# Attention with agents and a cosine FFN: one more lot of queries in the second and third burst of a batch

## The chip, the cores and the metric

One core of one Trainium2 chip runs the kernel. The metric is the time of one execution on the device, in microseconds; of the kernel before three runs are shown, 1187.72 to 1188.53 us, median 1188.37 us.

## The reference

For each of 4 batches there are 12480 queries, keys and values of 128 elements, and 49 agent vectors. `sm(a, b)` is the softmax over b of the scaled products of a and b.

```python
a2k = sm(agents, k)          # 49 x 12480
agent_v = a2k @ v            # 49 x 128
q2a = sm(q, agents)          # 12480 x 49
x = q2a @ agent_v            # attention output, 12480 x 128 per batch
h = x @ w_in                 # 49920 x 2048
out = (h * cos(h)) @ w_out   # 49920 x 128
```

## The kernel before

The queries of all batches are worked in 52 groups of 960, 13 a batch. In place of x, the kernel folds `agent_v @ w_in` into a matrix `a` for each batch (`project`, line 334), so that one product of the transposed softmax weights `pT` with `a` gives h.

**The steps.** The main loop (lines 807 to 829) has 16 steps a group, 832 in all. Step n computes two matmuls of 113 x 480 into a PSUM tile `ph` of two banks (L771, three such tiles), a Sin on ACT into `c` (L774), a scalar_tensor_tensor on DVE that makes `r` = (c - 1) * h (L780, called the cubic step here), and, four steps later (`LAG`), two matmuls of `r` with `w_out` (L796), accumulated over eight steps in a PSUM tile `one`. The last of eight adds two matmuls with `b1` and `b2` (L792, L793) and a copy to `osb` (L798); every 16 steps a group of the output goes to memory. There are two tiles `one`; one of them holds these output sums nearly all the time, the other serves everything else.

**The lots.** All that a later group or batch needs is done in between, in lots that hang on steps. A lot of **queries** (`query_parts`, line 415) loads 480 KB of transposed queries on SP (tile `xt`, three buffers), multiplies them by the agents (8 matmuls at L139, each in two passes, so 16 in the trace) into the free `one`, copies the scores to `e` (L432: on ACT, or on DVE where `by_vector` is set), takes the maxima on DVE (L436) and subtracts them on POOL (L438). A lot of **keys** (`scores`, line 221) is alike, with a running maximum on DVE. A lot of **values** (`add_values`, line 490) adds the exponentials to `es` on POOL (L283), loads twice 240 KB on SP (tile `vt`, six buffers), multiplies them by the exponentials of the keys (L297, 16 passes) into the free `one`, and adds that to `sums` on DVE (L305; the first lot copies, L303). A **turned** group (`query_turned`, line 501) transposes a group's weights on PE (L505), copies on ACT (L509) and writes `pT` on POOL (L512, L513). Each of the steps outside the bursts that are free takes at most one lot: `extra` (line 621) looks for the next of three steps in eight (five where `dense`).

**The bursts.** Exp and Sin need different tables on ACT, so the Exps are gathered: three bursts a batch, at steps 109, 133 and 157 from the batch's start (`BURSTS`, line 527). At a burst ACT loads the Exp table, runs one Exp over a piece of 4 or 5 query groups (L480) and one over 4 or 5 lots of keys (L273), and loads the Sin table at the next L774. DVE then sums the query groups (`query_sum`, L483), and five steps on computes their inverse (`query_inverse`, L487 and L488). For the six steps of a burst PE, DVE and ACT keep the order in which the code is written (`as_traced`, line 89).

`fill` (line 667) puts up to three lots into a burst and reserves its first three steps: the first lot whole at the burst's own step, two of the sums and then the second lot one step on (the other sums behind it), the matmuls of the third lot at the second step and the rest of it at the third. A query within a burst has its copy on DVE. Here the burst's steps put a lot ahead of `second_product`, and the cubic step of step n comes at step n + 1, after `first_product`.

Lines 708 to 735 hand out the lots of batch `b`'s keys and values (b = 1 to 3) and of the coming queries. `fresh[k]` lists the queries for burst k: four for the first, three that are left of five for the second (two go out before it), and the first two of the next batch for the third. `vs` lists the values: four for the second burst, four and then five for the third. The string of line 713 says in which order `fill` gets them; what it does not take is spread over the steps up to the next burst, or put every two to six steps after the third. After the values come the total, the folding, the inverse and the four projections of the batch (lines 736 to 742), and then the lots of the next batch's keys.

Of the kernel before, what the change touches and what calls it, by code (L numbers as in the profile page):

```python
# [41 lines left out]
def agent_attention_cos_ffn(ctx, tc, qT, kT, v, agT, w_in, w_out, outT):  # L42
# [338 lines left out]
    with ExitStack() as pools:  # L381
# [239 lines left out]
        def extra(n, f, *args, dense=False):  # L621


            while n in taken or (n - LAG) % NP not in ((1, 2, 3, 4, 5) if dense else (1, 3, 5)):
                n += 1
            taken.add(n)
            plan(n, f, *args)
            return n
# [5 lines left out]
        def spread_out(todo, t, end):  # L634

            for i, lot in enumerate(todo):
                t = extra(t, *lot) + 1
                if i + 1 < len(todo):
                    t += max(0, (end - t) // (len(todo) - i - 1) - 1)
            return t  # L640
# [14 lines left out]
        def burst(t, piece, keys=None):  # L655
            assert t + 4 < piece[0] * STEP - 10
            windows.add(t)
            plan(t, query_exp, piece)
            if keys:
                plan(t, pinned_exp, *keys)  # L660
            sums.extend((n, t) for n in piece)
            plan(t + 5, query_inverse, piece)

        def scored(piece, *how):
            return [(query, n, piece, *how) for n in piece]

        def fill(at, todo):

            taken.update(range(at, at + 3))
            parts = [in_parts(*todo.pop(0)) for _ in range(min(3, len(todo)))]  # L670
            if parts:
                plan(at, list, parts[0])
            early_plan(at + 1, summed, at, 2)
            if len(parts) > 1:
                early_plan(at + 1, list, parts[1])
            early_plan(at + 1, summed, at, 9)
            for x, n in zip(parts[2:], range(at + 2, at + 9)):
                early_plan(n, next, x)
                (early_plan if n + 1 < at + 5 else plan)(n + 1, list, x)
# [7 lines left out]
        for b in range(1, NB):  # L687
            o, ps = (b - 1) * PER, pieces[b - 1]

            def valued(k):  # L690
                return [(add_values, ab[b], g) for g in range(lots[k][0], sum(lots[k]))]

            qs, ks = scored(ps[0])[ahead:], [(ab[b].scores, g) for g in range(3 if b == 1 else 0, NG)]
            both = []
            while qs or ks:
                both += ks[:3] + qs[:1]
                ks, qs = ks[3:], qs[1:]
            t = spread_out(both, t, o + BURSTS[0] - 14)
            plan(t, ab[b].top)
            t = extra(t, ab[b].across)  # L700
            t = extra(t + 1, ab[b].spread)
            assert t < o + BURSTS[0], (t, o)
            for g, n in lots:
                plan(t, ab[b].shift, g, n, nc.gpsimd)
            nxt = scored(pieces[b][0], False, True)[:2]
            ahead = len(nxt)
            fresh = [scored(ps[1], False, True), scored(ps[2], False, True), nxt]
            for k, at in enumerate(BURSTS):
                at += o
                burst(at, ps[k], (ab[b], *lots[k]))  # L710
                vs, qs = valued(k - 1) if k else [], fresh[k]
                todo = []
                for x in ("qqqqqqq", "vq", "vq")[k]:
                    z = vs if x == "v" else qs
                    if z:
                        todo.append(z.pop(0))
                fill(at, todo)
                t = at + 6
                if k == 2:
                    vs += valued(2)  # L720
                qs, todo = todo, []
                qs += [x for x in fresh[k] if x not in qs]
                qs = [x[:3] if x[0] is query else x for x in qs]
                while vs or qs:
                    todo += qs[:1] + vs[:1]
                    vs, qs = vs[1:], qs[1:]
                if k == 0:
                    todo += [x[:3] for x in fresh[1][:2]]
                    del fresh[1][:2]
                end = o + BURSTS[min(k + 1, 2)] - 4  # L730
                for i, x in enumerate(todo):
                    t = extra(t, *x, dense=k == 2) + (2 if k == 2 else 1)
                    assert k == 2 or x[0] is not query or t < o + BURSTS[k + 1], (t, o, k)
                    if k < 2 and i + 1 < len(todo):
                        t += max(0, (end - t) // (len(todo) - i - 1) - 1)
            plan(t, ab[b].total)
            t = extra(t, ab[b].folded) + 1
            t = extra(t, ab[b].inverse) + 1
            i = b % 2
            for c in range(DFF // 512):  # L740
                t = extra(t, ab[b].project, c, a[i], dense=True) + 1
            t = extra(t, ab[b].project_out, wio, b1[i], b2[i], dense=True)
            plan(t, ab[b].judge)
            t += 1
            assert t < o + PER + 2, (t, o + PER)
# [229 lines left out]
```

## Time and profile before

| What | us |
|---|---|
| Median of three runs | 1188.37 |
| The profiled execution's own time | 1186.01 |
| Its span | 1184.2 |
| PE / DVE / ACT / POOL busy | 1129.3 / 1073.1 / 970.0 / 349.9 |
| Cubic steps on DVE (L780), 832 of them, busy | 916.4 |
| Sin on ACT (L774), 832 of them, busy | 785.4 |

The profile is that of one execution. The page sums it up by engine and by line; a timeline lists the instructions of an engine in order of time (start, duration, engine, line, operation, tiles, count, and in brackets the idle time before it with what ended it); windows give the busy time of every engine in a stretch of the span, with the number of instructions, the mean granted clock of TensorE (1.00 is 2.4 GHz) and the share of the DMA engines. Matmuls that follow each other overlap in the records, so a duration of one is longer than its place in the stream.

### The profile page before, as it was taken

How to read it: one execution, taken by the hardware profiler on the slowest of the kernel's cores; microseconds unless marked ns; L12 is line 12 of the kernel's file. 1: busy time of each engine (PE TensorE's matmuls, PEld its weight loads, DVE VectorE, ACT ScalarE, POOL GpSimd, SP SyncE). 2: the span in 40 equal slices, each digit the busy share in tenths (PEclk: the TensorE clock that was granted, in tenths of full speed). 3: DMA queues.
4: the chain of work that ended last, by engine and by line, in shares of the span. 5: the costliest groups of instructions: out<-in, count | busy, mean ns of one | idle time of the engine just before them, and what ended most of it. 6: DMA issues, size and time to landing. Idle time of an engine off the chain costs nothing.

```text
span 1184.2 us, 17390 instructions
## 1 busy us (share of the span) xinstructions
PE 1129.3 (95%) x6359; PEld 917.0 (77%) x6359; DVE 1073.1 (91%) x1220; ACT 970.0 (82%) x1201; POOL 349.9 (30%) x387
## 2 busy tenths in 40 slices
PE   8899999999999999998899999999999999998997
PEld 7678889777777888887677888878777777666774
DVE  6879999999889999998789999999878999999997
ACT  2568888888778888888778888888777899998996
POOL 1022221743313231373313231263332232122320
PEclk9899999999999999999899999999989999998999
DMA  9983233333341223233342222233331000000001
GB/s 340 246 244 100 85 100 100 101 100 95 106 134 50 84 68 100 68 101 100 100 134 68 84 70 88 82 97 106 95 100 35 34 17 34 34 18 34 18 34 37
DMA packets 39190, 107.74 MB, mean 91 GB/s; under 512 B 4344, under 2 KB 4728, under 8 KB 39096
## 3 DMA queue, kind: packets, MB, share of 16 engines
q1 hardware_dynamic: 39096, 106.55, 28.4%
q8 instruction: 52, 0.85, 0.3%
q14 instruction: 42, 0.34, 0.1%
HBM read 80.97 MB, written 25.56 MB: 90 GB/s over the span
## 4 chain that ended last, share of the span: by engine, by line
PE 67%; DVE 17%; ACT 8%; issue 4%; DMA 3%; POOL 0%; SPq 0%; ACTq 0%; DVEq 0%
PE ph L771 25%; PE one L796 22%; DVE r L780 14%; PE one L139 10%; ACT c L774 5%; PE one L297 3%; PE one L792 2%; PE one L793 1%; PE one L505 1%; DMA vt<-w_out 1%; DMA vt<-v 1%; PE one L342 1%; ACT osb L798 1%; ACT L480 1%; ACT s L273 1%
## 5 line engine op out<-in xcount | busy, mean ns | idle before, releaser
L780 DVE SCALAR_TENSOR_TENSOR r<-c,ph 128x960 fp32r<-128x960 f32 x832 | 916.4, 1148 | 62.9 <-ACT c L774 56.6
L774 ACT ACTIVATE c<-ph 128x960 f32<-128x960 f32 x832 | 785.4, 980 | 111.5 <-PE ph L771 99.0
L771 PE MATMUL ph<-pT,a 113*128 113x480 f32 x1664 | 540.7, 405 | 22.9 <-DVE r L780 21.6
L796 PE MATMUL one<-r,w 128*128 128x480 f32 x1664 | 504.0, 391 | 2.0 <-ACT osb L798 1.7
L771 PEld LDWEIGHTS ph<-pT,a 113*128 113x128 f32 x1664 | 293.0, 191 | 137.8 <-DVE r L780 73.3
L796 PEld LDWEIGHTS one<-r,w 128*128 128x128 f32 x1664 | 311.7, 192 | 55.5 <-issue 4.8
L139 PEld LDWEIGHTS one<-ag,xt 128*120 128x120 f32 x1408 | 162.8, 187 | 14.1 <-DVE sums L303 4.2
L139 PE MATMUL one<-ag,xt 128*120 128x49 f32 x1408 | 159.3, 266 | 5.4 <-DVE sums L303 2.9
L496 POOL TENSOR_TENSOR p<-e,rz 120x392 f32<-120x392 f32 x51 | 43.2, 851 | 328.0 <-PE one L505 252.5
L513 POOL TENSOR_TENSOR pT<-p,pT 49x480 fp32r<-49x480 f32 x102 | 124.1, 1217 | 7.8
L438 POOL TENSOR_TENSOR e<-e,mx 120x392 f32<-120x392 f32 x49 | 41.3, 843 | 212.8 <-DVE mx L436 212.3
L512 POOL CAST pT<-p 49x480 fp32r<-49x480 f32 x102 | 59.3, 582 | 115.0 <-ACT p L509 110.3
L798 ACT COPY osb<-one 128x480 f32<-128x480 f32 x104 | 57.9, 557 | 4.0 <-PE one L796 4.0
L297 PE MATMUL one<-vt,s 120*49 120x128 f32 (+1 forms) x624 | 44.6, 288 | 5.2 <-DVE sums L305 5.2
L297 PEld LDWEIGHTS one<-vt,s 120*49 120x49 f32 (+1 forms) x624 | 34.7, 135 | 18.0 <-issue 8.1
L283 POOL TENSOR_TENSOR es<-es,s 120x392 f32<-120x392 f32 x36 | 36.8, 1021 | 37.3 <-ACT s L273 35.7
L269 POOL TENSOR_TENSOR s<-s,mxb 120x1568 f32<-120x1568 f32 (+1 forms) x9 | 31.5, 3531 | 34.1 <-DVE mxb L265 34.1
L793 PE MATMUL one<-pT,b 113*128 113x480 f32 x104 | 40.3, 388 | 0.0
L792 PE MATMUL one<-pT,b 113*128 113x480 f32 x104 | 40.3, 387 | 0.0
L235 ACT COPY s<-one 120x392 f32<-120x392 f32 x36 | 17.5, 487 | 20.7 <-PE one L139 20.7
L432 ACT COPY e<-one 120x392 f32<-120x392 f32 x34 | 16.5, 487 | 20.3 <-PE one L139 20.3
L505 PEld LDWEIGHTS one<-ident,p 120*113 120x113 f32 x204 | 28.6, 179 | 4.7 <-ACT a L343 0.9
(105 smaller groups left out, 551.1 us busy)
## 6 DMA issues: line engine op xcount, KB each, us to landing
xt<-qT SPq DMA_DIRECT2D x52, 480.0 KB, 3.5
vt<-v SPq DMA_DIRECT2D x104, 240.0 KB, 3.5
outT<-osb SPq DMA_DIRECT2D x51, 480.0 KB, 2.6
xt<-kT SPq DMA_DIRECT2D x46, 480.0 KB, 3.5
c<-kT SPq DMA_DIRECT2D x6, 480.0 KB, 7.5
vt<-w_in SPq DMA_DIRECT2D x8, 256.0 KB, 7.1
vt<-w_out SPq DMA_DIRECT2D x8, 256.0 KB, 7.6
outT<-osb SPq DMA_DIRECT2D x2, 240.0 KB, 2.8
```

The lines of the kernel that those rows point to most:

```text
L139: mm = nc.tensor.matmul(ps[:, t, :], xt[:, t * TT:(t + 1) * TT], ag[:, b, :], start=True, stop=True)
L297: mm = nc.tensor.matmul(po[h * HI:h * HI + width], e[:, x * NA:x * NA + width], vt[:, x, :], start=(t == 0 and first), stop=(t == HT - 1 a ...
L496: nc.gpsimd.tensor_mul(p_in[n % 2].rearrange("p t (h a) -> p h t a", h=2)[:, :, :, :NA], e.rearrange("p (h t) a -> p h t a", h=2), rz_of.p ...
L512: nc.gpsimd.tensor_copy(pT[own, c], p[own])
L513: nc.gpsimd.tensor_sub(pT[other, c], p[own], pT[own, c].bitcast(F32))
L771: nc.tensor.matmul(ph[:, j, :CH], ai[:, f], pTs[q % 3][:, c], start=True, stop=True)
L774: nc.scalar.activation(cos, h, AF.Sin, bias=HALF_PI, scale=1.0)
L780: nc.vector.scalar_tensor_tensor(r, cos, 1.0, h, op0=ALU.subtract, op1=ALU.mult)
L792: nc.tensor.matmul(po, b1[k], pTs[q % 3][:, c], start=False, stop=False)
L793: nc.tensor.matmul(po, b2[k], pTs[q % 3][:, c], start=False, stop=False)
L796: nc.tensor.matmul(po, w1[:, f, :], r[:, j, :], start=(f == 0), stop=(f == NF - 1))
L798: nc.scalar.copy(osb[:, c * CH:(c + 1) * CH], po)
```

## The change

The strings of line 713 for the second and the third burst get a query ahead. `fill` then receives three lots in place of two at these bursts: a query at the burst's own step, values one step on, a query at the second and third step. What is left for the steps after is one query less; all that is handed out after it takes the place before its own. No lot is added or left out. The copy of the query that moves into a burst goes from ACT to DVE (`by_vector`).

```diff
@@ -710,7 +710,7 @@
                 burst(at, ps[k], (ab[b], *lots[k]))
                 vs, qs = valued(k - 1) if k else [], fresh[k]
                 todo = []
-                for x in ("qqqqqqq", "vq", "vq")[k]:
+                for x in ("qqqqqqq", "qvq", "qvq")[k]:
                     z = vs if x == "v" else qs
                     if z:
                         todo.append(z.pop(0))
```

## Rows read from the trace of the kernel before

**Rows 1.** The page: busy times by engine (part 1), issues of DMA (part 6).

```profile
PE 1129.3 (95%) x6359; PEld 917.0 (77%) x6359; DVE 1073.1 (91%) x1220; ACT 970.0 (82%) x1201; POOL 349.9 (30%) x387
...
xt<-qT SPq DMA_DIRECT2D x52, 480.0 KB, 3.5
```

**Rows 2.** Windows of eight steps at a burst; columns: stretch, length, busy by engine, clock.

```profile
503.87:519.05 15.18, 14.33 (x86) 11.33 (x86) 14.00 (x21) 13.46 (x13) 13.21 (x13) 1.00 0.42 131
257.86:272.50 14.64, 13.12 (x71) 10.91 (x71) 12.69 (x18) 13.52 (x14) 9.20 (x10) 0.88 0.24 71
539.18:554.85 15.67, 12.63 (x66) 10.59 (x66) 12.54 (x18) 13.65 (x14) 9.19 (x10) 0.89 0.22 67
823.67:840.04 16.37, 13.33 (x71) 11.29 (x71) 13.11 (x18) 13.66 (x15) 9.23 (x10) 0.90 0.21 63
294.11:311.25 17.14, 14.12 (x83) 12.05 (x84) 12.81 (x20) 13.84 (x13) 5.88 (x6) 0.90 0.36 115
577.00:595.39 18.39, 15.37 (x80) 12.92 (x81) 13.07 (x20) 14.03 (x13) 5.89 (x6) 0.81 0.33 107
861.56:880.30 18.74, 16.90 (x83) 14.55 (x84) 12.83 (x20) 13.94 (x13) 5.88 (x6) 0.73 0.35 106
```

**Rows 3.** Windows of eight steps outside the bursts.

```profile
954.59:963.36 8.77, 8.42 (x34) 5.92 (x34) 8.60 (x9) 7.74 (x10) 0.00 (x0) 1.00 0.14 56
...
554.85:566.03 11.18, 11.11 (x73) 9.30 (x73) 9.81 (x10) 8.40 (x10) 0.84 (x1) 1.00 0.41 132
272.50:283.14 10.64, 10.57 (x68) 8.75 (x68) 9.69 (x11) 8.41 (x10) 0.84 (x1) 1.00 0.42 140
283.14:294.11 10.97, 10.07 (x69) 7.77 (x68) 9.69 (x11) 9.09 (x12) 5.20 (x6) 1.00 0.31 90
...
322.59:333.34 10.75, 10.75 (x82) 8.43 (x81) 9.43 (x12) 7.71 (x9) 0.00 (x0) 1.00 0.56 182
333.34:343.48 10.14, 10.14 (x71) 8.17 (x71) 9.24 (x11) 8.12 (x10) 4.38 (x5) 1.00 0.35 102
311.25:322.59 11.34, 11.02 (x75) 8.74 (x75) 9.62 (x11) 8.86 (x11) 5.21 (x6) 1.00 0.30 87
595.39:607.04 11.65, 11.33 (x78) 9.04 (x78) 9.73 (x11) 8.87 (x11) 5.22 (x6) 1.00 0.28 86
```

**Rows 4.** Timeline, second burst of batch 2, DVE and PE; last column: idle before.

```profile
541.80 1.03 DVE L483 TENSOR_REDUCE rz<-e 120x8 f32<-120x392 f32 x2 [1.27 <-ACT e L480]
...
540.59 1.88 PE L139 MATMUL one<-ag,xt 128*120 128x49 f32 x16 [0.99 <-DVE sums L303]
...
546.79 0.68 PE L771 MATMUL ph<-pT,a 113*128 113x480 f32 x2 [2.06 <-DVE r L780]
```

**Rows 5.** Timeline, first burst of batch 2, PE and DVE.

```profile
505.55 1.88 PE L139 MATMUL one<-ag,xt 128*120 128x49 f32 x16 [0.66 <-DVE e L432]
...
512.30 0.56 DVE L432 COPY e<-one 120x392 f32<-120x392 f32 x1
...
513.45 3.27 DVE L780 SCALAR_TENSOR_TENSOR r<-c,ph 128x960 fp32r<-128x960 f32 x3
```

**Rows 6.** Timeline, third burst of batch 1, PE and DVE.

```profile
295.51 1.94 PE L297 MATMUL one<-vt,s 120*64 120x128 f32 x16 [1.72 <-DVE sums L305]
...
297.51 0.29 DVE L305 TENSOR_TENSOR sums<-sums,one 113x128 f32<-113x128 f32 x1 [2.05 <-PE one L297]
...
300.90 0.56 DVE L432 COPY e<-one 120x392 f32<-120x392 f32 x1 [2.17 <-PE one L139]
...
303.45 5.41 DVE L780 SCALAR_TENSOR_TENSOR r<-c,ph 128x960 fp32r<-128x960 f32 x5
```

**Rows 7.** L487: durations (ns min/median/max), then DVE and POOL at one of them.

```profile
L487 DVE TENSOR_SCALAR rz<-rz x12: 106/178/1000, 115.8 to 1075.1; 120x32 f32<-120x32 f32 x7, 120x40 f32<-120x40 f32 x4, 120x8 f32<-120x8 f32 x1
...
836.79 1.00 DVE L487 TENSOR_SCALAR rz<-rz 120x32 f32<-120x32 f32 x1
...
835.23 2.52 POOL L513 TENSOR_TENSOR pT<-p,pT 49x480 fp32r<-49x480 f32 x2
```

## The prediction

> **What bounds the kernel now.** I began with the busy times of the page: PE 95% of the span [rows 1], DVE and ACT less. Such a share says little of a burst, so I cut the DVE row into blocks of eight steps, each from the start of the cubic step L780 at one n to the one eight later, and asked for the busy times and the granted clock of each block. The plan's arithmetic (lines 690 to 745) says which lots stand in a block.
>
> Outside the bursts [rows 3] the blocks are regular. With no lot a block takes 8.77 us; that is eight cubic steps on DVE back to back. With three lots of values it takes 10.75, with two of values and a turned group 10.14; one query and one lot of values make 10.64, the same with a turned group 10.97 (11.34 and 11.65 after the third burst). PE is busy for 92 to 100% of all of these. So a block with two or more lots is paced by PE, and a lot costs what it costs there: values (10.75 - 8.77) / 3 = 0.66, and a query 10.97 - 8.77 - 0.66 = 1.5.
>
> A block that starts at a burst [rows 2] is another thing. The first burst of a batch, which holds three queries, takes 15.18 us with PE busy for 14.33 of it at granted clock 1.00 (batch 2; batch 3 gives the same, batch 1 half a microsecond more). The second burst holds less work, one lot of values and one query and a turned group, and takes 14.64, 15.67 and 16.37 in the three batches: PE is busy for 13.12, 12.63 and 13.33, at a mean clock of 0.88 to 0.90. The third takes 17.14, 18.39 and 18.74 at 0.90, 0.81 and 0.73. A mean of 0.88 over 14.64 us is 0.12 / 0.5 x 14.64 = 3.5 us at the lower of the two levels, 1.2 GHz.
>
> What holds PE up is seen in the order of the second burst [rows 4]. While ACT loads the Exp table, runs two Exps and loads Sin again, the only cubic steps that can run are those whose cosine is there. PE waits 0.99 us for the DVE copy that frees the PSUM buffer of the values (there is one such buffer: the other of the two holds the output sums), and then 2.06 us for an L780, because the ph buffers are full and it has no lot left. DVE has nothing either for 1.27 us, until the first Exp. In the first burst [rows 5] the same place has a third query; PE waits 0.66 us and nothing like the 2.06, and DVE pays for the third query behind two cubic steps: its copy begins at 512.30 and, the reduce done, the next cubic step at 513.45, so 1.15 us.
>
> **The change part by part.** Six bursts change, two in each of three batches; the first burst does not.
>
> *Second burst, inside.* The query now comes ahead of the values, and a second query two steps on. Each query issues one load of 480 KB on SP, eight matmuls, on DVE a PSUM copy in place of ACT's and a reduce (1.15 us together), and a POOL subtraction. The first copy and reduce fall into the 1.27 us in which DVE waits for Exp; the values' add, 0.29 us in [rows 6], follows the first two sums. DVE goes on when the cosine of the next step is there, as now; the second query then costs 1.15 us behind the next two cubic steps, as in the first burst. On PE its eight matmuls, 1.88 us in [rows 4], take the place of the 2.06 us wait. I price the block by the nearest rows: the first burst's 15.18 and 0.2 for the turned group that it lacks, 15.4 in every batch. Bounds: 15.0 with the values lighter than the query that they stand for, and 17.5, the worst of now (16.37) with the whole 1.15 on top. Against now: +0.8, -0.3, -1.0, together **-0.5**. The load is an early one: SP already holds the loads of the queries ahead, three buffers deep, and after the first burst it serves three queries in this spacing; I cost it at nothing, covered by those buffers, and at up to a load's 3.5 us [rows 1] per burst if they run dry; no load was waited for there in the first burst, so I stay at nothing. Loads of values that stand behind it on SP have six buffers; outputs have two.
>
> *Second burst, outside.* In the block after the burst the remaining query moves up to the place of the one that left, and a lot of values to the place after: one of each, as now. So 10.6, which takes 0.6 off in batch 2 alone (11.18 now, behind the slow clock). The block after that loses its query and keeps one lot of values and a turned group: 8.77 + 0.66 = 9.43 against 10.97, -1.54 in each of three batches, **-4.6**. If only DVE counted, the gain would be the reduce alone, under half of the 1.15 above; that is the lower bound.
>
> *Third burst, inside.* Here the last lot of values of the stretch before falls on the burst's own step, ahead of Exp, and the burst's first lot has to wait for its buffer: 1.7 us on PE [rows 6]. That stays, with a query as the one that waits. In batch 1 DVE now adds the second lot's sums at 297.51, waits 2.17 us for the query's matmuls, copies at 300.90, and starts the next cubic step only at 303.45. After: the query's matmuls start at 295.5 and end at about 297.7, copy and reduce to 299.1, two sums to 300.1; the values' matmuls run beside these, their add ends at 300.6, three sums to 302.0, then the cubic step, 1.45 us sooner. The new query's 1.15 comes two steps on. So 17.14 - 1.45 + 1.15 = 16.8 at full clock. The wait of 1.7 us that comes ahead of the low clock is still there, so I take 17.0 in all three. Bounds 15.7 (the new query hidden: 17.14 - 1.45) and 19.9 (18.74 and 1.15). Against now: -0.1, -1.4, -1.7, together **-3.3**.
>
> *Third burst, outside.* The next block swaps its query for values: 10.14 against 11.34, 11.65 and 11.34, **-3.9**. All later lots move up one place; at the end of the chain one place of values is gone, 0.66 a batch, **-2.0**. Total, inverse and the four projections of the next batch only come earlier, by two to six steps; the work that needs them starts long after, so nothing for that.
>
> The sum: -0.5 - 0.6 - 4.6 - 3.3 - 3.9 - 2.0 = **-14.9 us**. The profiled execution took 1186.0 us, 1184.2 of it span, so 1171.1 for it; the median of the runs shown lies 2.4 us above it, at 1188.4, so **1174 us** with some of the rounding against me.
>
> *A rule against it.* The reciprocal's first half (L487) reads and writes SBUF on DVE five steps into each burst. It took 1.00 us at 836.79 and ended 0.04 us after POOL's pair of L513 did, where 0.178 is its median [rows 7]. The change puts one more POOL subtraction ahead of that place. If L487 meets a POOL instruction in all six bursts, 6 x (1.00 - 0.18) = 4.9 us. The Trainium skill, page "SBUF — State Buffer", section "SBUF: two separate sides", says why: VectorE and GpSimd share a pair of ports that one instruction holds to its end while the other is blocked. By that rule the sum would be -10.0; by the rows, in which some bursts already pay for it, -14.9.
>
> **The rivals.** *The third lot only stacks up (1184).* Each block keeps its time and clock of now and DVE pays 1.15 on top: 6 x 1.15 = +6.9 inside in place of -3.8, and -11.1 outside: -4.2. For it: DVE's own sum rises, as a copy moves from ACT to it. Against it: the first burst [rows 2] does more in less time.
>
> *The port pair decides (1178.5).* As priced above.
>
> *One free PSUM buffer makes it slower (1198).* Three lots in a burst pass through one buffer. The second query's matmuls wait for the values' add, which stands on DVE behind two sums that wait for Exp; behind them on PE wait the second product and the next first product, so ACT has no input when its table is back. Its price would be the 1.72 us that a lot waits today [rows 6] and its own 1.7: 3.4 us a burst, 20.5 in six, less the 11.1 gained outside: +9.4. It decides from 11.1 / 6 = 1.85 us a burst on. For it: the low clock of the third burst [rows 2] follows just such a wait. The Trainium skill has it as a rule, page "TensorE: Matmul & The Clock Gate", section "A second HAM failure mode: psum-queue depth-cycling": short PE idles between groups that cycle through PSUM make its clock go up and down. Against it: three lots in a row at the first burst ran at 1.00 throughout.
>
> That the edit does nothing is excluded: the second burst's list holds three queries and the third's two, so each order finds its lots.
>
> **How the numbers follow.** Forecast 0.55; stacking 0.18; the ports 0.08; the buffer 0.12; the remaining 0.07 is for prices near the buffer's point of balance, where nothing is left to see. A measurement of this kernel tells some 0.2% (2.4 us) from no change. So faster 0.81, same 0.07, slower 0.12. The range: from 1167, where the six bursts come to their lower bounds (3 x 0.4 and 3 x 1.3 below the sum), to 1187, which takes in the ports and stacking, with a late load or two (3.5 us each at most) on top.
>
> **What would show it.** Right: blocks of the second burst near 15.4 at clock 1.00, PE's 2.06 us wait gone, 9.4 in the block that now takes 10.97, the cubic step after the third burst about 1.4 us sooner. Wrong: PE waiting for the values' add in the second burst by over 1 us, ACT waiting for L771 just after its Sin table, a mean clock under 0.9 in the second bursts, or the blocks of [rows 3] not shorter with a query less.

## The result, and the profile after

The changed kernel takes 1172.09 us (median of four runs, 1170.62 to 1173.21) where the kernel before takes 1188.45 beside it: ratio 0.9861, 95% interval 0.9844 to 0.9878, so 16.4 us less. The forecast was 1174 and its range 1167 to 1187. In a second measurement, against 17 runs of the kernel before, the same kernel gave 0.9889 (0.9846 to 0.9933), 13 us less (run `r_after` below). The profiled execution has a span of 1169.8 us, 14.4 less than before.

The blocks of eight steps, cut in the same way as in [rows 2, 3] (columns: stretch, length, busy time by engine with instructions, granted clock, DMA): the three second bursts and the three third bursts, the blocks that follow these, and the last links of the first batch's chain. Those of the other batches, where only one stands, agree with it to 0.1 us.

```profile
258.51:274.72 16.21, 14.18 (x91) 11.39 (x91) 14.14 (x21) 14.13 (x15) 10.13 (x11) 1.00 0.33 95
535.77:551.98 16.21, 14.18 (x91) 11.38 (x91) 14.15 (x21) 14.14 (x15) 10.14 (x11) 1.00 0.32 94
814.49:830.69 16.20, 14.18 (x91) 11.39 (x91) 14.14 (x20) 14.12 (x15) 10.13 (x11) 1.00 0.33 95
293.85:309.72 15.87, 14.47 (x103) 12.26 (x104) 13.76 (x23) 13.70 (x13) 6.77 (x7) 1.00 0.50 156
571.12:588.49 17.37, 15.98 (x103) 13.42 (x104) 13.94 (x23) 13.76 (x14) 6.78 (x7) 0.90 0.48 143
849.83:868.74 18.91, 17.51 (x103) 15.01 (x104) 13.94 (x23) 13.77 (x14) 6.77 (x7) 0.82 0.43 131
...
551.98:561.60 9.62, 9.57 (x66) 7.35 (x64) 9.43 (x12) 7.96 (x9) 0.85 (x1) 1.00 0.48 153
...
561.60:571.12 9.52, 8.90 (x52) 7.03 (x52) 9.05 (x10) 8.42 (x11) 4.45 (x5) 1.00 0.19 53
...
309.72:319.84 10.12, 10.12 (x70) 8.01 (x70) 9.19 (x12) 8.29 (x10) 4.39 (x5) 1.00 0.34 100
...
340.75:351.23 10.48, 10.34 (x45) 7.46 (x43) 9.99 (x16) 8.61 (x10) 0.19 (x1) 1.00 0.27 95
351.23:363.00 11.77, 11.58 (x51) 8.55 (x50) 11.14 (x13) 10.57 (x15) 6.71 (x9) 1.00 0.00 0
363.00:373.35 10.35, 10.12 (x63) 8.58 (x62) 9.18 (x11) 8.16 (x10) 0.13 (x1) 1.00 0.28 97
```

Every second burst now takes 16.2 us at clock 1.00, in place of 14.64, 15.67 and 16.37 at 0.88 to 0.90 [rows 2]: longer or alike, not shorter. Of the two blocks after it, the first takes 9.6 in place of 10.55 to 11.18 (10.55 in batch 3; the others stand in [rows 3]), the second 9.5 in place of 10.97. The third bursts take 15.87, 17.37 and 18.91 where they took 17.14, 18.39 and 18.74; the clock is still down in two of them. The block after takes 10.1 in place of 11.34 to 11.65. Over all blocks the two traces differ by 14.9 us, and the beginning gives 0.6 back. The last burst of the kernel, which the change does not touch, holds 0.8 us of it: its low clock lasted less long this time (mean 0.88 against 0.77).

The second burst of batch 2 in order of time (start, duration, engine, line, idle before), on DVE, PE and POOL, to be read beside [rows 4]; the last line is from the trace of the kernel before:

```profile
536.83 0.56 DVE L432 COPY e<-one 120x392 f32<-120x392 f32 x1
...
538.38 1.03 DVE L483 TENSOR_REDUCE rz<-e 120x8 f32<-120x392 f32 x2 [0.33 <-ACT e L480]
...
542.07 2.22 DVE L780 SCALAR_TENSOR_TENSOR r<-c,ph 128x960 fp32r<-128x960 f32 x2 [1.53 <-ACT c L774]
544.21 0.56 DVE L432 COPY e<-one 120x392 f32<-120x392 f32 x1
...
548.54 1.18 DVE L487 TENSOR_SCALAR rz<-rz 120x32 f32<-120x32 f32 x1
...
537.44 1.09 PE L297 MATMUL one<-vt,s 120*64 120x128 f32 x16 [0.78 <-DVE e L432]
...
539.66 1.88 PE L139 MATMUL one<-ag,xt 128*120 128x49 f32 x16
...
543.28 0.70 PE L771 MATMUL ph<-pT,a 113*128 113x480 f32 x2 [0.36 <-DVE r L780]
544.82 0.67 PE L505 MATMUL one<-ident,p 120*113 120x120 f32 x4 [0.84 <-DVE e L432]
...
548.47 2.50 POOL L513 TENSOR_TENSOR pT<-p,pT 49x480 fp32r<-49x480 f32 x2
...
545.49 4.35 DVE L780 SCALAR_TENSOR_TENSOR r<-c,ph 128x960 fp32r<-128x960 f32 x4 [0.58 <-ACT c L774]
```

The query's copy stands at 536.83, in the time in which DVE waited for Exp: of that wait of 1.27 us, 0.33 is left. But DVE gets nothing for it: its wait for the first cosine after the Sin table, 0.58 us before, is now 1.53, and from the start of the block to that cubic step it is 6.3 us in both kernels (545.49 - 539.18 and 542.07 - 535.77). PE's 2.06 us for an L780 became 0.36, since the second query's matmuls stand ahead of it (539.66). New is a wait of 0.84 us of the turned group for the second query's copy, and L487 takes 1.18 us where [rows 7] have 1.00 as the longest: it runs beside the first of POOL's pair of L513 and ends with it, half-way through the pair's 2.50 us.

The third burst of batch 1, on PE and DVE, beside [rows 6]:

```profile
295.25 1.88 PE L139 MATMUL one<-ag,xt 128*120 128x49 f32 x16 [1.93 <-DVE sums L305]
...
297.16 0.57 DVE L432 COPY e<-one 120x392 f32<-120x392 f32 x1 [1.97 <-PE one L139]
...
299.25 0.28 DVE L305 TENSOR_TENSOR sums<-sums,one 113x128 f32<-113x128 f32 x1
...
300.85 2.21 DVE L780 SCALAR_TENSOR_TENSOR r<-c,ph 128x960 fp32r<-128x960 f32 x2
```

From the end of PE's wait to the first cubic step after the burst it was 303.45 - 295.51 = 7.9 us; it is 300.85 - 295.25 = 5.6, with the wait ahead of it still there (1.93 us, 1.72 before).

### The profile page after: what moved, and what is told of

Its sections match the earlier page's. It is cut to its first block, busy times and chain, and to the rows that moved or that the text cites. A ratio compares the mean times of both kernels' runs of the same rounds, so it can differ in the third digit from the quotient of the medians.

```text
span 1169.8 us, 17396 instructions
## 1 busy us (share of the span) xinstructions
PE 1121.8 (96%) x6359; PEld 911.8 (78%) x6359; DVE 1075.4 (92%) x1226; ACT 967.6 (83%) x1195; POOL 351.0 (30%) x387
## 4 chain that ended last, share of the span: by engine, by line
PE 68%; DVE 17%; ACT 8%; issue 5%; DMA 1%; POOL 0%; SPq 0%; ACTq 0%; DVEq 0%
PE ph L771 26%; PE one L796 22%; DVE r L780 13%; PE one L139 9%; ACT c L774 5%; PE one L297 3%; PE one L793 2%; PE one L792 2%; PE one L505 1%; PE ph L149 1%; PE one L342 1%; ACT osb L798 1%; ACT L480 1%; ACT s L273 1%; DMA vt<-w_out 1%
## 5 line engine op out<-in xcount | busy, mean ns | idle before, releaser
L780 DVE SCALAR_TENSOR_TENSOR r<-c,ph 128x960 fp32r<-128x960 f32 x832 | 915.3, 1148 | 52.2 <-ACT c L774 44.7
L771 PE MATMUL ph<-pT,a 113*128 113x480 f32 x1664 | 533.8, 401 | 14.4 <-DVE r L780 12.2
L796 PEld LDWEIGHTS one<-r,w 128*128 128x128 f32 x1664 | 307.8, 189 | 51.8 <-issue 4.5
L513 POOL TENSOR_TENSOR pT<-p,pT 49x480 fp32r<-49x480 f32 x102 | 124.3, 1219 | 7.8
L297 PEld LDWEIGHTS one<-vt,s 120*49 120x49 f32 (+1 forms) x624 | 34.4, 134 | 16.2 <-issue 8.1
L505 PE MATMUL one<-ident,p 120*113 120x120 f32 x204 | 29.8, 268 | 2.5 <-DVE e L432 2.5
```

Of the source, the lines that this page charges most:

```text
L297: mm = nc.tensor.matmul(po[h * HI:h * HI + width], e[:, x * NA:x * NA + width], vt[:, x, :], start=(t == 0 and first), stop=(t == HT - 1 a ...
L505: mm = nc.tensor.transpose(pt[:KR, t * TT:(t + 1) * TT], p_in[n % 2][:, t, :KR], ident[:TT, :TT])
L513: nc.gpsimd.tensor_sub(pT[other, c], p[own], pT[own, c].bitcast(F32))
L771: nc.tensor.matmul(ph[:, j, :CH], ai[:, f], pTs[q % 3][:, c], start=True, stop=True)
L780: nc.vector.scalar_tensor_tensor(r, cos, 1.0, h, op0=ALU.subtract, op1=ALU.mult)
L796: nc.tensor.matmul(po, w1[:, f, :], r[:, j, :], start=(f == 0), stop=(f == NF - 1))
```

## The experiments

All but the filler are edits of line 713 or of the plan; every kernel does the whole work. The runs form three groups (`e1` to `e4`; `r_after` and `e5` to `e7`; `e8` to `e11`), each on a chip and against runs of the kernel before of its own. So ratios are compared, and what a run saves against the kernel before is worked out from its ratio.

**Each half alone.** The second or the third burst keeps its two lots.

```diff
-for x in ("qqqqqqq", "qvq", "qvq")[k]:
+for x in ("qqqqqqq", "qvq", "vq")[k]:      # e1_second_only
+for x in ("qqqqqqq", "vq", "qvq")[k]:      # e2_third_only
```

> Only the second bursts take the extra query. Theory (each lot that moves into a burst fills PE time that was a wait, and leaves a block that PE paces): the second bursts' blocks at 16.2 us, clock 1.00, the two blocks after them at 9.6 and 9.5; about -6 us against the kernel before, so 1182. Rival (the lot stacks up in the burst, and the gain of the change comes from the third bursts): -1 us or less, 1187 to 1189.

> Only the third bursts take the extra query. Theory: the third bursts' blocks and the ones after them as in the changed kernel, -7 to -8 us, so 1180 to 1181; together with the other half it makes up the whole. Rival (the two halves gain only together, as the second burst's half lets the third start from a clock that is up): under -5 us.

Measured: 0.9941 (0.9924 to 0.9958), 7.0 us, for the second bursts alone; 0.9956 (0.9935 to 0.9978), 5.2 us, for the third alone. The sum, 12.2, is 0.9897 of the time, and `r_after` with 0.9889 does not differ from it: the halves add, as far as the intervals tell. So the gain is not the third bursts' alone, and the rival of the first run is out. The rival of the second (under 5 us alone) is not: 5.2 us, where 7 to 8 were expected, has an interval of 2.6 to 7.7. In its three third bursts the clock fell each time, in the six of the two traces of the changed kernel four times, which is too few to tell whether the one half helps the other. The windows of the first kernel, then of the second, show why one profile is not enough here:

```profile
536.35:552.56 16.21, 14.18 (x91) 11.38 (x91) 14.14 (x20) 14.14 (x15) 10.13 (x11) 1.00 0.33 94
...
292.88:308.44 15.56, 12.55 (x83) 10.74 (x84) 12.89 (x20) 13.71 (x13) 5.91 (x6) 1.00 0.39 127
571.70:590.44 18.74, 17.04 (x83) 14.64 (x83) 12.82 (x21) 13.95 (x13) 5.88 (x6) 0.73 0.32 105
```

```profile
259.10:273.75 14.65, 13.00 (x71) 10.79 (x71) 12.69 (x19) 13.53 (x14) 9.21 (x10) 0.88 0.25 71
540.29:554.92 14.63, 11.58 (x71) 9.88 (x71) 12.67 (x18) 13.53 (x14) 9.19 (x10) 1.00 0.25 71
819.95:834.59 14.64, 13.16 (x71) 11.23 (x71) 12.78 (x19) 13.52 (x14) 9.19 (x10) 0.88 0.24 71
295.36:314.34 18.98, 17.58 (x103) 15.02 (x104) 13.94 (x22) 13.76 (x14) 6.75 (x7) 0.82 0.42 130
576.56:593.93 17.37, 15.97 (x103) 13.46 (x104) 14.03 (x22) 13.75 (x14) 6.76 (x7) 0.90 0.49 143
```

Blocks whose code is that of the kernel before take other times in another execution: its third burst 15.56 at clock 1.00 and 18.74 at 0.73 (293 and 572 in the first fence), its second burst 14.63 to 14.65 (second fence) where [rows 2] have up to 16.37. At full clock, then, the kernel before needs 14.6 and 15.6 for these blocks, less than the changed one with 16.2 and 15.9.

The mean clock of a block does not say by itself what it costs. In the second fence the second bursts at 0.88 take the same 14.6 us as the one at 1.00. Where the low clock falls counts; the three second bursts of the kernel before show it when they are cut 7.1 us after their start. These are the windows of the later parts:

```profile
264.96:272.50 7.54, 7.04 (x43) 6.39 (x44) 7.54 (x9) 6.46 (x9) 6.25 (x7) 1.00 0.00 1
546.28:554.85 8.57, 8.06 (x38) 7.08 (x39) 7.39 (x9) 6.59 (x9) 6.24 (x7) 0.80 0.01 3
830.77:840.04 9.27, 8.76 (x43) 7.79 (x44) 7.97 (x9) 6.60 (x10) 6.28 (x7) 0.82 0.00 1
```

In batch 1 all of the low clock lies in the first part, in which DVE waits for Exp, and the block is as short as at full clock. In the other two it lies in the later part, which is 1.0 and 1.7 us longer, and by as much the whole block is. So what [rows 2] have above 14.6 and 15.6 is read here as the price of the low clock; no run holds the clock still to prove it.

> The changed kernel itself, on the chip and against the runs of the kernel before that the next three share. Ratio 0.984 to 0.990 as in the first measurement; mean granted clock 0.986 to 0.991 against 0.978 to 0.985. If the two halves measured alone (0.9941 and 0.9956) only add up, 0.990; if they help each other, 0.986 or below.

Measured: 0.9889, clock 0.988 to 0.992 in its four runs against a median of 0.981 of the kernel before. It agrees with the sum of the halves, 0.9897; whether they help each other a little, these intervals do not tell.

**Only the clock.** The kernel before, with PE work that nobody needs in the place of its wait:

```diff
+filled = {b * PER + at + x for b in range(NB - 1) for at in BURSTS[1:] for x in (2, 3)}
 nc.tensor.matmul(ph[:, j, :CH], ai[:, f], pTs[q % 3][:, c], start=True, stop=True)
+if n in filled:
+    for _ in range(2):
+        nc.tensor.matmul(ph[:, j, :CH], ai[:, f], pTs[q % 3][:, c], start=True, stop=True)
```

> The kernel before; in its second and third bursts the first product's matmuls of the third and fourth step are issued three times each, 8 matmuls more per burst, with the same result and no lot moved. Theory (the moved lot is what counts; the clock costs little by itself): -2 to +1 us, 1186 to 1189, although the granted clock of the second bursts goes up to 1.00. Rival (the gain is the clock's, and any PE work in the wait brings it): -5 us or more, 1183 or below.

Measured: 0.9971 (0.9951 to 0.9992), 3.4 us faster with 48 matmuls more and no lot moved. That lies between the two expectations: the clock alone is worth something, and my theory had it at nothing. The windows (two second, two third bursts):

```profile
543.14:558.76 15.62, 14.64 (x79) 12.63 (x79) 12.74 (x18) 13.54 (x14) 9.32 (x10) 0.89 0.25 67
828.22:842.89 14.67, 13.37 (x79) 11.42 (x79) 12.71 (x18) 13.52 (x14) 9.23 (x10) 1.00 0.26 71
295.20:315.38 20.18, 18.77 (x93) 16.58 (x93) 13.09 (x20) 13.75 (x13) 5.90 (x6) 0.75 0.30 98
...
864.49:880.05 15.56, 14.16 (x91) 12.24 (x92) 12.90 (x20) 13.94 (x13) 5.93 (x6) 1.00 0.37 126
```

Second bursts come to 1.00 in two of three batches; third bursts with the low clock stand at 20 us, above the 17.1 to 18.7 of [rows 2], since there it follows the wait for the values' sums, ahead of the filler, which is then more work at the low clock. Over the ten runs, time and mean clock go together: 1174.37 us at 0.995, 1184.88 at 0.982, so 10.5 us for 0.013.

**The order.** Three lots, values first.

```diff
-("qqqqqqq", "qvq", "qvq")
+("qqqqqqq", "vqq", "vqq")
```

> Three lots in each of these bursts as in the changed kernel, in the order values, query, query. Theory (the number of lots brings most, and the first place only decides whether the query's copy and reduce, 1.15 us, fall into DVE's wait for Exp): 1 us more per second burst than the changed kernel, 1172 to 1177. Rival (a query ahead of the values is what matters, since the second query has to wait for the one free PSUM buffer otherwise): 1180 or above.

Measured: 1.0006 (0.9976 to 1.0035): nothing is left of the gain, as the rival had it, though not for its reason. The profiled execution was the fastest of its ten runs (1177.11 us at clock 0.984; the slowest took 1191.39 at 0.969). In it the second bursts at full clock take the same 16.2 us as with the query first, so the query's copy in DVE's wait is worth nothing by itself. A third burst at clock 1.00 takes 16.64, 0.8 us more than the changed kernel's 15.87. The rest of the difference goes with the clock. The second burst of batch 3 and the third of batch 2 (windows), then from the timeline the latter's PE and ACT rows:

```profile
818.61:836.44 17.83, 16.85 (x89) 14.77 (x89) 14.44 (x20) 14.01 (x15) 10.01 (x11) 0.81 0.31 85
...
570.65:592.62 21.97, 20.57 (x103) 18.05 (x104) 14.40 (x22) 13.94 (x14) 6.71 (x7) 0.69 0.36 113
```

```profile
572.05 1.09 PE L297 MATMUL one<-vt,s 120*64 120x128 f32 x16 [1.93 <-DVE sums L305]
...
574.58 3.28 PE L139 MATMUL one<-ag,xt 128*120 128x49 f32 x16
...
584.45 0.97 ACT L774 ACTIVATE c<-ph 128x960 f32<-128x960 f32 x1 [3.84 <-PE ph L771]
```

Two lots of values stand beside the wait of 1.93 us; after them the clock is 0.69 on average, a query's matmuls take 3.28 us in place of 1.88, ACT waits 3.84 us, and the block takes 22 us. Median clock of the ten runs: 0.975, where the order with the query first has 0.989 (`r_after`).

**L487 and the port pair.** The inverse eight steps after the burst's start:

```diff
-plan(t + 5, query_inverse, piece)
+plan(t + 8, query_inverse, piece)
```

> The changed kernel with the inverse of the query sums eight steps after the burst's start in place of five, where POOL has finished the turned group. Theory of the port pair (L487 took 1.18 us in the second bursts because it meets POOL's L513): L487 back to 0.2 us there, the second bursts' blocks at 15.2 and the whole 2 to 3 us faster than the changed kernel. Rival (PE has by then a lead of its own, and DVE catches up): L487 at 0.2 us and the time the same within 1 us.

Measured: 0.9927 (0.9901 to 0.9954), 1177.14 us, 4.2 us slower than `r_after` with 1172.94; its fastest run (1173.26) lies above the slowest there (1173.03). Neither side expected a loss. The longest L487 is now 0.178 us; its group (durations in ns), and in windows the second burst with the block behind it:

```profile
L487 DVE TENSOR_SCALAR rz<-rz x12: 107/174/178, 119.6 to 1070.3; 120x32 f32<-120x32 f32 x7, 120x40 f32<-120x40 f32 x4, 120x8 f32<-120x8 f32 x1
```

```profile
540.18:555.12 14.94, 12.91 (x84) 10.20 (x83) 12.88 (x18) 13.66 (x14) 9.88 (x11) 1.00 0.37 103
...
555.12:566.38 11.26, 10.84 (x74) 8.54 (x73) 9.82 (x13) 8.52 (x10) 1.10 (x2) 1.00 0.40 131
```

The burst's block is 1.27 us shorter (14.94, with 84 matmuls in place of 91), and the one after it 1.64 longer (11.26, with 74 in place of 66): while L487 stood, PE went on, and that lead paid for the next query. So in the two blocks together no price of the port shows, 25.83 us with it and 26.20 without. The later place also moves the inverse into the second of these blocks, so the run does not price the port alone. The move itself costs 0.3 to 0.5 us a burst over the blocks around it, and it is made in all of them.

**The values clear of the third burst.** Lots between the second and the third burst closer together:

```diff
-end = o + BURSTS[min(k + 1, 2)] - 4
+end = o + BURSTS[min(k + 1, 2)] - (12 if k == 1 else 4)
```

> The changed kernel with the lots between the second and the third burst closer together, so that the last lot of values no longer stands on the third burst's own step. Theory (what is left to gain is the wait of 1.9 us for its sums and the low clock after it): no such wait, third bursts' blocks at 15.2 to 15.6 and clock 1.00, the stretch before 0.7 us longer per batch; 3 to 5 us faster than the changed kernel, about 1168 where it has 1172. Rival (another lot waits there for the one free PSUM buffer all the same): within 1 us of the changed kernel.

> The changed kernel with both edits, the later inverse and the values clear of the third burst. Theory: the two gains add, 5 to 8 us faster than the changed kernel. Rival: no more than the second edit alone.

> The changed kernel with the values clear of the third burst once more, in more rounds, to see whether it beats the changed kernel (ratio 0.986 to 0.989 to the kernel before in two measurements). Theory: ratio 0.985 to 0.988, 1168 to 1171 us, mean clock 0.993 and above in most runs. Rival: no better than the changed kernel, 1172 to 1174 us.

Measured: 0.9873 (0.9825 to 0.9921), 1169.91 us, and in the third group 0.9868 (0.9844 to 0.9891), 1170.41; with the late inverse as well 0.9914, 1175.37, so that edit costs here too. The wait for the sums is down from 1.93 us to 0.37 (PE rows of the third burst of batch 2), and all three third bursts take 15.83 at clock 1.00 (windows, with the two blocks after the second burst):

```profile
574.08 1.09 PE L297 MATMUL one<-vt,s 120*64 120x128 f32 x16 [0.67 <-DVE e L432]
...
576.62 1.88 PE L139 MATMUL one<-ag,xt 128*120 128x49 f32 x16 [0.37 <-DVE sums L305]
```

```profile
572.41:588.24 15.83, 13.98 (x88) 10.05 (x88) 13.65 (x22) 14.02 (x13) 6.80 (x7) 1.00 0.41 126
850.55:866.39 15.84, 14.01 (x88) 10.04 (x88) 13.66 (x22) 14.03 (x13) 6.83 (x7) 1.00 0.40 125
...
552.28:563.19 10.91, 10.91 (x83) 8.37 (x82) 9.69 (x12) 7.91 (x9) 0.85 (x1) 1.00 0.56 177
...
563.19:572.41 9.22, 9.14 (x53) 7.80 (x52) 9.05 (x11) 8.42 (x11) 4.43 (x5) 1.00 0.20 59
```

That is no shorter than the changed kernel's 15.87 at full clock; what is gained is that the clock stays up, here and in the traces of `e7` to `e9` and `e11`. The price is 1.0 us a batch (10.91 and 9.22 after the second burst in place of 9.62 and 9.52). Against `r_after` of the same group it is 3.0 us faster, with intervals that overlap, so by the times alone it is not settled that it beats the changed kernel; in the blocks the gain is plain. It has the lowest times here.

> The kernel before (two lots in these bursts), with the last lot of values moved off the third burst's own step by the one edit that made the changed kernel faster there. Theory (the clock and the moved lots are two gains of like size; this edit gets a part of the first without any of the second): the wait of 1.7 us gone, third bursts at 15.0 to 16.5 in place of 17.1 to 18.7, 3 to 5 us faster than the kernel before; the bursts still fall to the lower clock after the wait for L780. Rival (the extra lot is needed to get anything): within 1 us of the kernel before.

Measured: the same edit on the kernel before, 0.9944 (0.9922 to 0.9966), 1178.73 us, 6.6 us less by the ratio (4.0 to 9.3), where 3 to 5 were expected. Its third bursts take 14.75 at clock 1.00, its second ones still 14.6 to 15.9 at 0.88 and 0.89. So 40 to 50% of what the change gained (16.4 and 13 us) can be had without moving a query into a burst. In its trace the low clock stands in a first burst too, whose code this edit leaves as it is: 19.7 us at 0.65 (batch 1), where the kernel before has 15.7 at 1.00.

**Values as the third lot, and a fourth lot,** both with the values clear:

```diff
-("qqqqqqq", "qvq", "qvq")
+("qqqqqqq", "qvv", "qvv")      # e9_qvv
+("qqq", "qvqv", "qvqv")        # e10_four_lots, fill: min(4, len(todo)), at + 4 reserved
```

> Three lots and the values clear of the third burst, but the third lot is values in place of a query. Theory (what a moved lot brings is the PE time that it takes out of a block paced by PE): the values take 1.1 us of PE where a query takes 1.6 to 1.9, and cost DVE 0.3 where a query costs 1.15; outside a query stays and a lot of values goes: 0 to 4 us slower than the same kernel with a query third (about 1170). Rival (DVE's 1.15 in the burst is what is left to save): 2 us or more faster, 1168 or below.

> Four lots in these bursts, query, values, query, values, with the values clear of the third burst. Theory (after the third lot PE has no wait left that a lot of 1.1 us fits into: 0.4 to 0.8 us each): within 2 us of the same kernel with three lots (about 1170). Rival (each further lot in a burst brings what the third did): 3 to 6 us faster.

Measured: values third 0.9896 (0.9862 to 0.9931), 1172.24 us, within the 0 to 4 us expected and not told apart from a query third. Its second bursts are shorter (14.56 in place of 16.2), the blocks after them longer by nearly as much (12.25 in place of 10.9). Four lots: 1.0006 (0.9986 to 1.0026), 1186.24 us: 16 us slower than `e11` with three lots, which neither side expected. The third burst of batch 2, its window and the PE and ACT rows of its timeline:

```profile
579.17:597.80 18.63, 14.92 (x101) 11.66 (x100) 14.21 (x22) 13.85 (x13) 6.77 (x7) 0.91 0.43 130
```

```profile
583.39 1.88 PE L139 MATMUL one<-ag,xt 128*120 128x49 f32 x16 [0.38 <-DVE sums L305]
...
588.88 1.09 PE L297 MATMUL one<-vt,s 120*64 120x128 f32 x16 [2.66 <-DVE e L432]
...
591.56 0.97 ACT L774 ACTIVATE c<-ph 128x960 f32<-128x960 f32 x1 [3.74 <-PE ph L771]
```

The fourth lot waits 2.66 us for the one free PSUM buffer: the third lot's copy stands on DVE behind two cubic steps, and these behind the Sin table. Behind the fourth lot on PE stand the first products, so ACT waits 3.74 us, and the clock falls (0.91). The one of these six bursts without a fall, a second one, took 17.57 us, still 1.4 more than with three lots; the other five took 18.6 to 19.1. That is the slower rival of the prediction, one lot later than it was feared.

## Why the prediction was right

**The sum held, several terms did not.** Term by term, block by block:

| Term | forecast, us | trace, us |
|---|---|---|
| Second bursts | -0.5 | +1.9 |
| Block after them | -0.6 | -3.5 |
| Next block | -4.6 | -4.3 |
| Third bursts | -3.3 | -2.1 |
| Block after them | -3.9 | -4.1 |
| End of the chain | -2.0 | -1.9 |
| Sum | -14.9 | -14.0 |

The step that failed is the price of the second burst, "the first burst's 15.18 and 0.2 for the turned group that it lacks, 15.4 in every batch". It is 16.2. From the first cosine after the Sin table to the end of the block DVE does not stand still, so that part is as long as DVE's work, and L487 takes 1.0 us more of it than in the first burst, whose time was taken (0.17 us there, batch 2). That price the prediction had worked out under the rule against it, and left out of the sum. The 0.84 us of the turned group are a wait of PE and do not make this block longer. But a cut at DVE's steps does not cut PE's work: in that time PE ran ahead, and the block that I left at 10.6 came out at 9.6. The two errors are one, and `e5` shows it, where the first vanishes and the second comes back. In the third bursts I took 17.0 for all; they take 15.87 at full clock and 17.4 or 18.9 where it falls, 17.4 on average. That 17.0 lies near this average is luck: no block takes it, and in another execution (`r_after`) they take 17.42, 15.87 and 17.36. Nor was the cubic step after the third burst 1.45 us sooner but 2.3, in batch 1, where the clock now stayed up.

**Outside the bursts** the prices were right to 0.3 us in each sum of three blocks: a block paced by PE gets shorter by what its lot costs PE. The load that was priced at nothing cost nothing: in the changed kernel no idle time of PE ahead of a query's matmuls ends with a load.

**The clock** had no line of its own in the sum; it stood in the terms of the bursts, and by estimate it is about half of the result. At full clock a batch's blocks of the kernel before take 14.64 + 10.64 + 10.97 = 36.25 us from the second burst to the third, the changed ones 16.21 + 9.62 + 9.52 = 35.35; from the third on it is 15.56 + 11.36 = 26.92 against 15.87 + 10.12 = 25.99, and the chain's end 0.6 less. That is 2.5 us a batch or 7.4 in all for the moved lots. The other half of the 14.4 is time at the low clock that no longer is: the bursts of [rows 2] hold 10.4 us above their times at full clock, those of the changed kernel 4.5, and the blocks behind them 0.7 less than before. These sums are of two executions, and another one of either kernel has others: 3.0 in the trace of `r_after`, and 5.9 for third bursts of the code of the kernel before in that of `e1`, where [rows 2] have 7.6. By the runs, 0.989 in the median against 0.981 is 0.008, and at the filler's 10.5 us for 0.013 this makes 6.5; the kernel before itself follows its mean clock less closely than that (last section). So the forecast owes its -14.9 in part to an execution of the kernel before in which the clock fell in all six bursts.

**The rivals.** Stacking alone is refuted by `e1` and `e2`. The port pair is there, as the Trainium skill has it (page "SBUF — State Buffer", section "SBUF: two separate sides"): L487 took 1.18 us beside POOL's L513 and 0.18 away from it. But of the six changed bursts it met one in the three second ones only, over a burst's block and the next no price of it shows (`e5`), and the rule's -10.0 did not come. The one free PSUM buffer did not decide with the query first; it does with the values first, by way of the clock, and with a fourth lot.

**What stays open.** Why the clock falls in one execution of a third burst and not in the next one of the same code no run settles. The gain of clearing the values over the changed kernel is measured to no better than some 3 us.

## What to carry to other kernels

Where an engine has to wait at a place that cannot be helped (here a pair of table loads), the work to put there is what the pacing engine needs, only as much as fits its wait, and in an order in which no piece waits for the buffer of the one before: a third lot brought 13 to 16 us, about half of it by way of the clock, and a fourth lost as much. Before more work goes into a gap, look for a lot that waits there already; taking one such out gave 40 to 50% of this gain by itself. A block cut at one engine's steps is to be summed with its neighbour before it is read as gain or loss, and a time of a PE-bound kernel is to be read beside its granted clock, block by block.

## What the runs showed that I had not expected

The time of one and the same kernel can go with the mean granted clock of the execution, over a range as wide as the effect studied: 1177.11 us at 0.984 to 1191.39 at 0.969 in `e4`, which is 14.3 us for 0.015, and 10.5 for 0.013 in `e3`. It does not always: of the kernel before, beside `e8`, one run took 1181.84 us at 0.979 and another 1185.80 at 0.988. The mean counts a low clock that costs nothing, as in the first of the second bursts above, like one that does. Work that is thrown away made the kernel before 3.4 us faster (0.9 to 5.8). And the same code of a third burst took 15.56 us at clock 1.00 and 18.74 at 0.73, in one and the same execution.
